# A planner's queue model, eight weight transfers and four chunk sizes in a fused attention and MLP kernel

## The chip, the cores and the metric

The kernel runs on one core of a Trainium2 chip. The metric is the device time in microseconds (us) of one execution. Five engines work side by side, each on its own stream of instructions in a fixed order: TensorE (PE: matmuls, with weight loads shown apart as PEld), VectorE (DVE), ScalarE (ACT), GpSimd (POOL) and SyncE (SP). SP computes nothing here; it issues transfers. Transfers issued by SP, ACT or POOL land later and announce it by semaphores. An instruction whose input is late holds up all that stand behind it on its engine.

## The reference

Inputs are q, k and v, each 8 batches x 8 heads x 576 positions x 64, in float32, and the MLP weights w_ch1 (512 x 2048) and w_ch2 (2048 x 512). Per head:

```
scores = q @ k.T / sqrt(64) + slope_h * (-|i - j|)
scores = where(0 <= i - j < 128, scores, -1e9)
attn   = softmax(scores) @ v
```

Heads are joined to x of 8 x 576 x 512, and then

```
xn  = (x - mean) / sqrt(var + 1e-6) * g_ln
out = x + relu(xn @ w_ch1) @ w_ch2
```

## The kernel before, in words

The 8 x 576 rows are 36 blocks of 128 positions. A block sees its own 128 keys and those of the block before. Nine blocks (`PERIOD`) make two batches; block 4 of the nine holds the end of one batch and the start of the next, so its q, k and v come as two half loads each.

For each block `attention(i)` records tasks. The names below are those that the prediction uses.

- SP loads q, k and v (256 KB each, `load`, L273) into rings of five buffers.
- POOL casts them to fp16: `cq`, `ck` (L369) and `cv` (L382).
- `T`: PE transposes q and k (L391), `ev` copies the result out of PSUM (L399 on DVE, L401 on ACT). From block `QK_BY_DMA` on, a DMA transpose issued by SP, `QT` (L406), stands for both.
- `S`: the scores (L426). For blocks below `BY_BIAS`, `Z` (L441) first writes the distance bias and the mask into PSUM by matmuls with a scaled identity; other blocks are masked after the exponential by `mk` (L472), a multiplication with a table.
- `ex`: the exponential on ACT (L465). `pv`: probabilities times v in two halves, `pva` and `pvb` (L489). `rc` and `nm` divide by the row sums (L505, L509), and `bn`, `ag` and `xs` give the normalised input of the MLP (L526 to L537).
- `TX`: PE transposes xs (L549), and `xt` copies it (L557, L559). From `X_BY_DMA` on, a DMA transpose `XT` (L564) stands for both.

Blocks are gathered in chunks (`CHUNKS`). For chunk c, `mlp(c)` records sixteen groups `Ac.f` of four matmuls each (L598; 128 columns of the moving operand per block of the chunk), each followed by a relu (L608 or L610), and then, for every block, four groups `Bi.0`, `Bi.4`, `Bi.8` and `Bi.12` of four matmuls (L624), `o` (L632), which adds x, and the output transfer (L640). Group `Ac.f` needs weight piece w(f // 4). Group `Bi.f` needs piece w(4 + f // 4). The eight pieces (L347, L349) are transfers that POOL issues, of 512 KB each as written, with a cast from float32. The PSUM banks `fb0` to `fb3` are shared by T, pv, TX, A and B.

The order of all instructions is not written by hand. `Plan.run` (L69) plays the tasks through a model of the engines. Each task has a guessed cost, dependencies and a due value `v`; `av(i, stage)` gives attention its due values. The order in which tasks start in the model is the order in which they are emitted, and so the order on every engine. Costs and times of the model are guesses and are not used as times in this text. A dependency that is named to the planner sets the order; only true data dependencies become semaphores. Before the change all transfers share one modelled queue `DMA`, one after the other, and a piece of weights may be issued as soon as a named load (`W_AFTER`) has landed in the model.

While the modelled start of a PE task is below `WARM` = 26, `keep_warm` (L651) fills the modelled gaps of PE with matmuls on a tile of zeros (L653).

Of the kernel before, what the change touches and what calls it, by code (L numbers as in the profile page):

```python
# [15 lines left out]
class Task:  # L16
    __slots__ = ("eng", "emit", "deps", "v", "lat", "acq", "rel", "left", "users", "ready", "end", "start", "name")

    def __init__(self, name, eng, emit, deps, v, lat, acq, rel):
        self.name, self.eng, self.emit, self.v, self.lat = name, eng, emit, v, lat  # L20
        self.deps = [d for d in deps if d is not None]
        self.acq, self.rel = acq, rel
        self.users, self.ready, self.end, self.start = [], 0.0, None, None

# [21 lines left out]
class Plan:  # L46


    def __init__(self):
        self.tasks, self.rings, self.banks, self.opens = [], [], {}, {}  # L50
# [5 lines left out]

    OVERLAP = {"ACT": 0.10, "DVE": 0.07, "POOL": 0.05}

    def add(self, name, eng, emit, deps=(), v=0.0, lat=None, acq=None, rel=None):
        if not isinstance(eng, dict):  # L60
            eng = dict([eng])
        if lat is None:
            lat = 0.2 if "PE" in eng else 0.05 + max(self.OVERLAP[e] for e in eng)
        eng = {e: c - self.OVERLAP.get(e, 0.0) for e, c in eng.items()}
        t = Task(name, eng, emit, deps, v, lat, acq, rel)
        self.tasks.append(t)
        return t

    def run(self):  # L69
        for r in self.rings:  # L70
            r.link()
        for t in self.tasks:
            t.left = len(t.deps)
            for d in t.deps:
                d.users.append(t)
        engines = sorted({e for t in self.tasks for e in t.eng})
        free = dict.fromkeys(engines, 0.0)
        avail = {e: [] for e in engines}
        for t in self.tasks:
            if t.left == 0:  # L80
                for e in t.eng:
                    avail[e].append(t)
        state = {p: {b: self.opens.get((p, b), 0.0) for b in bs} for p, bs in self.banks.items()}
        held, waits = {}, {}
        for t in self.tasks:
            if t.rel is not None:
                waits[t.rel] = waits.get(t.rel, 0) + 1
        order = []

        def at(t):  # L90
            if t.acq is None or t.acq[1] in held:
                return t.ready, None
            open_ = [(when, b) for b, when in state[t.acq[0]].items() if when is not None]
            if not open_:
                return None, None
            when, b = min(open_)
            return max(t.ready, when), b

        left = len(self.tasks)
        while left:  # L100
            best = None
            for e in engines:
                f = free[e]
                cand = []
                for t in avail[e]:
                    r, b = at(t)
                    if r is None:
                        continue
                    s = max(r, f)
                    if any(max(r, free[o]) + c < s + t.eng[e] - 1e-9 for o, c in t.eng.items() if o != e):  # L110
                        continue
                    cand.append((s, t.v, t, b))
                if not cand:
                    continue
                s = min(c[0] for c in cand)
                c = min((c for c in cand if c[0] <= s + 1e-9), key=lambda c: (c[2].v > -9e3, c[2].ready) if e == "DMA" else c[1])
                if best is None or (s, c[1]) < (best[0], best[1]):
                    best = (s, c[1], e, c[2], c[3])
            if best is None:
                raise RuntimeError("plan is stuck: " + ", ".join(t.name for e in engines for t in avail[e])[:600])  # L120
            s, _, e, t, b = best
            for o in t.eng:
                avail[o].remove(t)
            t.start, t.end = s, s + t.eng[e]
            free[e] = t.end
            if t.acq is not None and t.acq[1] not in held:
                held[t.acq[1]] = (t.acq[0], b)
                state[t.acq[0]][b] = None
            if t.rel is not None:
                waits[t.rel] -= 1  # L130
                if waits[t.rel] == 0:
                    p, hb = held[t.rel]
                    state[p][hb] = t.end + t.lat
            order.append((t, e, held[t.acq[1]][1] if t.acq is not None else None))
            left -= 1
            for u in t.users:
                u.ready = max(u.ready, t.end + t.lat)
                u.left -= 1
                if u.left == 0:
                    for o in u.eng:  # L140
                        avail[o].append(u)
        self.held = held
        self.order = order
        return order


@with_exitstack
def kernel(
# [10 lines left out]
    nc = tc.nc  # L159
# [4 lines left out]
    P = 128  # L164
# [7 lines left out]
    CH = CB * P  # L172
    CHUNKS = [3, 3, 2, 4, 4, 4, 4, 4, 4, 4]
    FIRST = [sum(CHUNKS[:c]) for c in range(len(CHUNKS))]
# [26 lines left out]
    WARM = 26.0  # L201
    PICK = {('xt', 0): 'ACT DVE', ('xt', 8): 'ACT DVE', ('cv', 5): 'ACT', ('cv', 0): 'POOL', ('ev', 8): 'DVE ACT', ('ev', 1): 'ACT', ('mkb', 8): 'POOL', ('mkb', 3): 'DVE', ('mka', 2): 'POOL'}
    G_AT = 1.3
    BY_BIAS = 4
    MASK_AT = 4
    QK_BY_DMA = 14
    X_BY_DMA = 14

    plan = Plan()
# [58 lines left out]

    def dma(name, eng, issue, secs, emit, deps=(), v=0.0):
        t = add(name + ".i", (eng, issue), emit, deps, v, lat=0.0)  # L270
        return t, add(name, ("DMA", secs), None, [t], -1e4 if eng == "POOL" else v, lat=2.0)

    def load(name, src, r, i, v):  # L273
        got = []
        for p0, n, b, s0 in where(i):
            def emit(e, bank, p0=p0, n=n, b=b, s0=s0):
# [3 lines left out]
                )  # L280
            t, d = dma(f"{name}{i}", "SP", 0.6, 1.22 * n / P, emit, (), v)
            r.writes(i, t)
# [7 lines left out]
    for t in vx.tiles:  # L290
        nc.vector.memset(t[:, :, D:VD], 1.0)

    d_iden = dma("iden", "ACT", 0.5, 0.15, lambda e, b: nc.scalar.dma_start(out=iden, in_=iden_dram.ap()), (), -1e6)[1]
    d_dist = dma("dist", "ACT", 0.5, 0.45, lambda e, b: nc.scalar.dma_start(out=dist_t, in_=dist_dram.ap()), (), -9e5)[1]
    d_g = dma(
        "g", "SP", 0.6, 0.8,
        lambda e, b: nc.sync.dma_start(out=g_t, in_=moe_g_ln.unsqueeze(0).broadcast_to([P, d_model])), (), av(G_AT) - 300,
# [3 lines left out]
    for h in range(H):  # L301
        def emit(e, b, h=h):
            nc.vector.tensor_scalar(out=sid[:, h, :], in0=iden[:, :], scalar1=-float(slopes[h] / inv_sqrt_d), scalar2=None, op0=ALU.mult)
# [36 lines left out]

    W_AFTER = [11, 14, 14, 17, 17, 17, 17, 17]
    t_w1, t_w2 = [], []
    for n, i in enumerate(W_AFTER):
        def emit(e, b, n=n):
            m = n % 4
            if n < 4:
                nc.gpsimd.dma_start(out=w1sb[:, :, 512 * m : 512 * m + 512], in_=w1r[:, :, 512 * m : 512 * m + 512])  # L347
            else:
                nc.gpsimd.dma_start(out=w2sb[:, 4 * m : 4 * m + 4, :], in_=w2r[:, 4 * m : 4 * m + 4, :])  # L349
        (t_w1 if n < 4 else t_w2).append(dma(f"w{n}", "POOL", 0.8, 3.25, emit, loads[i // 3][i % 3], av(i / 3, -60.0))[1])  # L350

    qkt_done, vx_done, aggr_done, xs_done, xt_done = {}, {}, {}, {}, {}

    def attention(i):
# [28 lines left out]
        cv = add(f"cv{i}", pick("cv", "POOL", POOL=0.64, ACT=0.62), e_cv, lv_, av(i, 0.2))  # L383
        v32.reads(i, cv); vx.writes(i, cv)

        if i < QK_BY_DMA:
# [17 lines left out]
        else:  # L404
            def e_td(e, b):
# [3 lines left out]
                )  # L409
            ti, ev = dma(f"QT{i}", "SP", 1.0, 1.1, e_td, [cq, ck], av(i, -4.0))  # L410
            qk16.reads(i, ev)
# [150 lines left out]
        else:  # L562
            def e_xd(e, b):
                nc.sync.dma_start_transpose(out=xt[c][:, :, j * P : j * P + P], in_=xs[i][:, :])  # L564
            xi, xt_ = dma(f"XT{i}", "SP", 1.0, 0.6, e_xd, [xs_], av(i, 7.0))
            xs.reads(i, xt_)
# [19 lines left out]
    def mlp(c):  # L586
# [5 lines left out]
        for f in range(NFB):  # L592
# [3 lines left out]
            def e_a(e, b, f=f):  # L596
                for kb in range(NKB):
# [3 lines left out]
                    )  # L601
            a = add(key, ("PE", 0.216 * nb), e_a, done + [t_w1[f // 4]], vm, acq=("fb", key))
            xt.reads(c, a)
# [10 lines left out]
        for j in range(nb):  # L614
# [3 lines left out]
            for f0 in range(0, NFB, 4):  # L618
                vm = v0 + 16 * per + (4 * j + f0 / 4) * SPAN / 32

                def e_b(e, b, j=j, f0=f0, key=key):
                    pm = fb[plan.held[key][1]]
                    for f in range(f0, f0 + 4):
# [3 lines left out]
                        )  # L627
                last = add(f"{key}.{f0}", ("PE", 0.864), e_b, relu[f0 : f0 + 4] + [t_w2[f0 // 4], last], vm, acq=("fb", key))
                ht.reads(c, last)
# [9 lines left out]
            def e_d(e, b, i=i):  # L639
                nc.sync.dma_start(out=out_flat[i * P : i * P + P, :], in_=ot[i][:, :])  # L640
            t, d = dma(f"out{i}", "SP", 0.6, 0.8, e_d, [o], vm - 4.0)
            ot.reads(i, d)
# [51 lines left out]
```

## Time and profile before

| what | value |
|---|---|
| median of 7 runs | 335.32 us (334.0 to 335.88) |
| the profiled execution | 334.71 us, of it 332.9 us of span |
| PE busy | 318.1 us, 96% of the span |
| DVE, ACT, POOL busy | 56%, 47%, 24% |
| granted PE clock over the span | 0.985 |
| MLP product one (L598) / two (L624) | 135.3 us / 132.2 us of PE |
| weight pieces, from issue to landing | w_ch1 8.0 us, w_ch2 14.3 us (medians of 4) |
| q, k, v loads of 256 KB, from issue to landing | 4.6, 4.8, 5.0 us (medians) |

The profile is of one execution; the span runs from its first to its last instruction. PE is busy nearly throughout, but its warm-up matmuls count as busy too, and a matmul at half clock is busy for twice as long. Tables by stretch tell more than the share of the whole. In a timeline row the columns are the start, the duration, the engine, the line, the operation, what it writes and reads, and how many; in brackets stands the idle time of the engine ahead of it, and what ended it.

### The profile page before, as it was taken

Reading aid. Unit: us, or ns where it says so; the run is one execution under the profiler, and the core shown is the slowest. Engines: PE = TensorE matmul, PEld = TensorE weight load, DVE = VectorE, ACT = ScalarE, POOL = GpSimd, SP = SyncE. Lnnn points to the kernel's source line nnn. Section 1 sums busy time; section 2 is a strip of 40 time slices with the busy share of each in tenths; the row PEclk is TensorE's granted clock in tenths of the full one; section 3 lists DMA queues with packets and bytes.
Section 4 is the critical chain, followed back from the end, with each engine's and each line's share of the span. In section 5 each row is a group of like instructions: output and inputs, shape, how many; then the busy total and the mean of one; then the engine's idle time right before and its main releaser. Section 6 shows DMA issues by size and latency. Waiting matters only on the chain.

```text
span 332.9 us, 6829 instructions
## 1 busy us (share of the span) xinstructions
PE 318.1 (96%) x2695; PEld 175.1 (53%) x2695; DVE 187.0 (56%) x403; ACT 156.6 (47%) x253; POOL 80.9 (24%) x127
## 2 busy tenths in 40 slices
PE   8996499999899999999999999999999999999994
PEld 8883355565586454554544444444445445444442
DVE  1597530389897655865666666666656655511011
ACT  4444362284383583457326722772277327505600
POOL 3881701507632213250131232132000000000000
PEclk9999599999999999999999999999999999999999
DMA  9999999998999999999999997623422320121011
GB/s 184 220 177 215 187 196 211 207 270 181 210 249 223 205 233 178 247 198 223 192 222 198 199 163 194 144 49 97 123 51 56 104 81 18 25 70 63 2 63 63
DMA packets 157584, 51.54 MB, mean 155 GB/s; under 512 B 148592, under 2 KB 152816, under 8 KB 157552
## 3 DMA queue, kind: packets, MB, share of 16 engines
q1 hardware_dynamic: 153040, 46.68, 69.3%
q0 software_dynamic: 4224, 4.19, 7.6%
q8 instruction: 21, 0.34, 0.5%
q10 hardware_dynamic: 288, 0.23, 0.2%
q14 instruction: 11, 0.09, 0.1%
HBM read 37.19 MB, written 9.44 MB: 140 GB/s over the span
## 4 chain that ended last, share of the span: by engine, by line
PE 87%; DVE 7%; DMA 4%; issue 1%; POOL 0%; DVEq 0%; POOLq 0%
PE fb L598 38%; PE fb L624 35%; PE sc L426 5%; PE fb L489 4%; DMA k<-in_k_dram 4%; PE fb L653 3%; DVE xs L537 2%; DVE st L526 1%; PE fb L391 1%; DVE xb L509 1%; PE fb L549 1%; DVE qkt L399 1%; DVE probs L472 1%; DVE ot L632 0%; PE sc L441 0%
## 5 line engine op out<-in xcount | busy, mean ns | idle before, releaser
L598 PE MATMUL fb<-xt,w1sb 128*128 128x512 f16 (+2 forms) x640 | 135.3, 361 | 0.2 <-DMA w1sb<-in_moe_w_ch_dram 0.2
L624 PE MATMUL fb<-w2sb,ht 128*128 128x512 f16 x576 | 132.2, 379 | 0.0
L610 ACT ACTIVATE ht<-fb 128x512 f16<-128x512 f32 (+2 forms) x145 | 80.4, 558 | 83.0 <-PE fb L598 82.3
L465 ACT ACTIVATE probs<-sc 128x1024 f16<-128x1024 f32 (+1 forms) x72 | 67.8, 973 | 52.5 <-PE sc L426 52.4
L598 PEld LDWEIGHTS <-w1sb 128*128 128x128 f16 x640 | 59.9, 98 | 57.0 <-issue 1.2
L624 PEld LDWEIGHTS <-ht 128*128 128x128 f16 x576 | 53.5, 98 | 59.2
L632 DVE SCALAR_TENSOR_TENSOR ot<-fb,rstd,xb 128x512 f32<-128x512 f32 x36 | 27.0, 749 | 68.7 <-PE fb L624 68.0
L382 POOL CAST vx<-v 128x512 f16<-128x512 f32 x35 | 22.0, 631 | 112.6 <-PE fb L489 96.2
L472 DVE TENSOR_TENSOR probs<-probs,mreg 128x1024 f16<-128x1024 f16 (+1 forms) x47 | 31.5, 675 | 18.1 <-ACT probs L465 17.9
L369 POOL CAST qk<-q 128x512 f16<-128x512 f32 x36 | 24.3, 674 | 37.5 <-issue 18.3
L509 DVE TENSOR_TENSOR xb<-fb,rec 128x256 f16<-128x256 f32 x72 | 30.2, 422 | 2.1
L537 DVE SCALAR_TENSOR_TENSOR xs<-xb,mv,g_t 128x512 f16<-128x512 f16 x36 | 29.8, 827 | 1.1
L489 PEld LDWEIGHTS <-probs 128*128 128x128 f16 x544 | 24.1, 98 | 11.6 <-DVE probs L472 0.8
L489 PE MATMUL fb<-vx,probs 128*128 128x65 f16 x544 | 26.8, 194 | 0.4 <-POOL probs L472 0.2
L369 POOL CAST qk<-k 128x512 f16<-128x512 f32 x36 | 23.7, 657 | 14.6 <-DMA k<-in_k_dram 14.5
L526 DVE BATCH_NORM_STATS2 st<-xb 128x6 f32<-128x512 f16 x36 | 24.9, 691 | 0.8
L505 DVE RECIPROCAL rec<-fb 128x4 f32<-128x4 f32 x72 | 12.7, 177 | 18.3 <-PE fb L489 17.9
L426 PEld LDWEIGHTS <-qkt 64*128 64x128 f16 x544 | 15.7, 95 | 11.7 <-issue 10.8
L426 PE MATMUL sc<-qkt 64*128 64x128 f16 x288 | 19.7, 219 | 0.0
L426 PE MATMUL sc<-qkt,qkt 64*128 64x128 f16 x256 | 18.4, 221 | 0.8 <-DVE qkt L399 0.8
L653 PE MATMUL fb<-warm_t 128*128 128x128 f16 x191 | 14.9, 240 | 1.0 <-DVE warm_t L288 1.0
L391 PE MATMUL fb<-iden,qk 128*128 128x128 f16 x112 | 9.1, 222 | 5.3 <-POOL qk L369 5.1
(35 smaller groups left out, 106.0 us busy)
## 6 DMA issues: line engine op xcount, KB each, us to landing
out_dram<-ot SPq DMA_DIRECT2D x36, 256.0 KB, 3.2
q<-in_q_dram SPq DMA_DIRECT2D x32, 256.0 KB, 4.6
k<-in_k_dram SPq DMA_DIRECT2D x32, 256.0 KB, 4.8
v<-in_v_dram SPq DMA_DIRECT2D x32, 256.0 KB, 5.0
w1sb<-in_moe_w_ch_dram POOLq DMA_DIRECT2D x4, 512.0 KB, 8.0
w2sb<-in_moe_w_ch_dram POOLq DMA_DIRECT2D x4, 512.0 KB, 14.3
q<-in_q_dram SPq DMA_DIRECT2D x8, 128.0 KB, 4.1
k<-in_k_dram SPq DMA_DIRECT2D x8, 128.0 KB, 3.6
```

The lines of the kernel that those rows point to most:

```text
L369: en.tensor_copy(out=qk16[i][:, a, :], in_=s)
L426: nc.tensor.matmul(scs[half][:, g, c0 : c0 + P], kt[rows, 1, hp, :], qkt[i][rows, 0, hp, :], start=not bias, stop=True, skip_group_check=True,
L465: nc.scalar.activation(out=o, in_=n_, func=AF.Exp, scale=inv_sqrt_d)
L472: en.tensor_tensor(out=pv, in0=pv, in1=mask[:, 2 * half : 2 * half + 2, :, lo:], op=ALU.mult)
L489: nc.tensor.matmul(pp[:, hh * (D + 1) : hh * (D + 1) + D + 1], probs[i][:, bank, slot, side * P : side * P + P], vx[i - 1 + side][:, h, 0 ...
L509: nc.vector.tensor_tensor(out=xb[i][:, 256 * half : 256 * half + 256].rearrange("p (h d) -> p h d", d=D), in0=pp[:, :, 0:D], in1=rec[2 * i ...
L526: nc.vector.bn_stats(out=st[i][:, :], in_=xb[i][:, :])
L537: nc.vector.scalar_tensor_tensor(out=xs[i][:, :], in0=xb[i][:, :], scalar=mv[c][:, j, 0:1], in1=g_t[:, :], op0=ALU.subtract, op1=ALU.mult,)
L598: nc.tensor.matmul(fb[b][:, 0:n_], w1sb[:, kb, f * P : f * P + P], xt[c][:, kb, 0:n_], start=(kb == 0), stop=(kb == NKB - 1),)
L610: nc.scalar.activation(out=ht[c][:, f, 0:n_], in_=src, func=AF.Relu)
L624: nc.tensor.matmul(pm[:, :], ht[c][:, f, j * P : j * P + P], w2sb[:, f, :], start=(f == 0), stop=(f == NFB - 1),)
L632: nc.vector.scalar_tensor_tensor(out=ot[i][:, :], in0=fb[plan.held[key][1]][:, :], scalar=rstd[c][:, j : j + 1], in1=xb[i][:, :], op0=ALU. ...
```

## The change

The planner's model of transfers is replaced. Each issuing engine has its own modelled queue, and queues that are active together share the rate by fixed parts. A transfer waits for room in its queue. The simulation steps through time with a heap of events, where before it chose the earliest start. `transfer` takes the place of `dma` at all call sites, with new costs:

```diff
+    QUEUE_ROOM = 4.0
+    LANDING = 2.0
...
+    def transfer(self, name, eng, issue, secs, room, emit, deps=(), v=0.0):
+
+        i = self.add(name + ".i", (eng, issue), emit, deps, v, lat=0.0)
+        d = self.add(name, ("DMA " + eng, secs), None, [i], v, lat=self.LANDING)
+        i.room = d.room = room
+        return i, d
+
+    def rates(self, queues):
+        on = [q for q, x in queues.items() if x]
+        if "DMA POOL" in on and len(on) > 1:
+            return {q: 0.92 if q == "DMA POOL" else 0.17 / (len(on) - 1) for q in on}
+        return {q: 1.0 / len(on) for q in on}
...
-    def dma(name, eng, issue, secs, emit, deps=(), v=0.0):
-        t = add(name + ".i", (eng, issue), emit, deps, v, lat=0.0)
-        return t, add(name, ("DMA", secs), None, [t], -1e4 if eng == "POOL" else v, lat=2.0)
...
-            t, d = dma(f"{name}{i}", "SP", 0.6, 1.22 * n / P, emit, (), v)
+            t, d = plan.transfer(f"{name}{i}", "SP", 0.6, 1.22 * n / P, n / P, emit, (), v)
...
-            ti, ev = dma(f"QT{i}", "SP", 1.0, 1.1, e_td, [cq, ck], av(i, -4.0))
+            ti, ev = plan.transfer(f"QT{i}", "SP", 1.4, 1.4, 1.0, e_td, [cq, ck], av(i, -4.0))
...
-            xi, xt_ = dma(f"XT{i}", "SP", 1.0, 0.6, e_xd, [xs_], av(i, 7.0))
+            xi, xt_ = plan.transfer(f"XT{i}", "SP", 1.2, 0.85, 0.5, e_xd, [xs_], av(i, 7.0))
...
-            t, d = dma(f"out{i}", "SP", 0.6, 0.8, e_d, [o], vm - 4.0)
+            t, d = plan.transfer(f"out{i}", "SP", 0.42, 0.8, 0.12, e_d, [o], vm - 4.0)
```

The core of the new loop:

```diff
+            for e in engines:
+                if free[e] > now + 1e-9:
+                    continue
+                best = None
+                for t in avail[e]:
+                    if best is not None and t.v >= best[0].v:
+                        continue
...
+                    if t.room and used["DMA " + e] + t.room > self.QUEUE_ROOM:
+                        continue
...
+            rate = self.rates(queues)
+            ends = [(now + queues[q][0][1] / r, q) for q, r in rate.items()]
...
+            nxt = min([x[0] for x in ends] + ([max(now, heap[0][0])] if heap else []))
+            for q, r in rate.items():
+                queues[q][0][1] -= (nxt - now) * r
```

The weight pieces are tied to casts in place of loads, and each comes after the piece before it. The constants change too:

```diff
-    W_AFTER = [11, 14, 14, 17, 17, 17, 17, 17]
...
-        (t_w1 if n < 4 else t_w2).append(dma(f"w{n}", "POOL", 0.8, 3.25, emit, loads[i // 3][i % 3], av(i / 3, -60.0))[1])
+    W_AFTER = [8, 14, 15, 15, 16, 17, 17, 18]
+    t_w = {}
+
+    def weights(i, casts):
+
+        for n, at in enumerate(W_AFTER):
+            if at // 3 != i:
+                continue
...
+            last = [t_w[n - 1][0]] if n else []
+            t_w[n] = plan.transfer(f"w{n}", "POOL", 0.8, 3.2, 0.0, emit, [casts[at % 3]] + last, av(i, -60.0))
...
         v32.reads(i, cv); vx.writes(i, cv)
+        weights(i, (cq, ck, cv))
...
-    CHUNKS = [3, 3, 2, 4, 4, 4, 4, 4, 4, 4]
+    CHUNKS = [2, 3, 4, 3, 4, 4, 4, 4, 4, 4]
...
-    PICK = {('xt', 0): 'ACT DVE', ('xt', 8): 'ACT DVE', ('cv', 5): 'ACT', ('cv', 0): 'POOL', ('ev', 8): 'DVE ACT', ('ev', 1): 'ACT', ('mkb', 8): 'POOL', ('mkb', 3): 'DVE', ('mka', 2): 'POOL'}
+    PICK = {('xt', 0): 'ACT DVE', ('xt', 8): 'ACT DVE', ('cv', 5): 'ACT', ('cv', 0): 'POOL ACT', ('ev', 8): 'DVE ACT', ('ev', 1): 'ACT', ('mkb', 8): 'POOL', ('mkb', 3): 'POOL', ('mka', 2): 'DVE', ('mkb', 4): 'POOL'}
     G_AT = 1.3
-    BY_BIAS = 4
-    MASK_AT = 4
-    QK_BY_DMA = 14
+    BY_BIAS = 6
+    MASK_AT = 6
+    QK_BY_DMA = 12
     X_BY_DMA = 14
```

An entry n of `W_AFTER` names block n // 3 and its q, k or v by n % 3. In the built order of the changed kernel POOL's stream from the first piece on reads cq4, w0, cq3, ck3, cv3, ck4, cv4, w1, cq5, w2, w3, ck5, w4, w5, w6, cq6, w7, ck6, cv6; before it read ck3, w0, cv3, cq4, ck4, w1, w2, cv4, cq5, ck5, w3 to w7, cq6, ck6, cv6. SP's loads read g, half of q4, q2, k2, v2, the other half of q4, half of k4, q3, k3, v3, the rest of k4, v4, then q5 and on; before, block after block. PE's order from the first MLP group reads A0.0, A0.1, TX2, pva3, A0.2, pvb3, Z4, T4, A0.3, S4, TX3, T5, pva4, pvb4, Z5, S5, A0.4; before, A0.0 to A0.3, pva4, TX3, pvb4, T5, S5, TX4, A0.4.

## The prediction

> **What bounds the kernel now.** I read the page's head first, then the busy time by stretch, then TensorE's timeline in the one stretch that looks bad, then the queues that feed it.
>
> ```profile
> span 332.9 us, 6829 instructions
> PE 318.1 (96%) x2695; PEld 175.1 (53%) x2695; DVE 187.0 (56%) x403; ACT 156.6 (47%) x253; POOL 80.9 (24%) x127
> ```
> ```profile
> 0.00:26.00 26.00, 24.24 (x403) 22.25 (x403) 14.04 (x47) 12.26 (x21) 16.45 (x28) 1.00 1.04 197
> 26.00:43.00 17.00, 9.49 (x82) 6.04 (x83) 9.88 (x20) 6.73 (x10) 8.14 (x11) 0.70 1.12 197
> 43.00:61.00 18.00, 18.00 (x109) 9.56 (x107) 3.11 (x8) 7.12 (x16) 3.17 (x6) 1.00 1.18 207
> 61.00:92.00 31.00, 29.58 (x327) 18.11 (x326) 25.70 (x55) 16.73 (x27) 15.50 (x21) 1.00 1.00 218
> 92.00:143.00 51.00, 51.00 (x463) 29.41 (x461) 36.01 (x76) 27.42 (x47) 12.92 (x22) 1.00 1.10 222
> 143.00:329.00 186.00, 185.78 (x1321) 89.73 (x1319) 97.70 (x200) 86.34 (x134) 24.73 (x41) 1.00 0.56 112
> ```
>
> The columns after each stretch are PE, PEld, DVE, ACT, POOL, granted clock, DMA share, GB/s. TensorE (PE) is the bound, and full from 92 us to the last matmul at 328.8; 4.1 us of tail follow. An order can gain only ahead of 92: the fill before 26 (mostly warm-up matmuls, L653), 26 to 43 (9.5 busy of 17, clock 0.70), and about 1.4 us idle in 61 to 92. A clock of 0.70 over 17 us is 0.30 x 17 x 2 = 10.2 us at half speed.
>
> ```profile
> 26.20 2.77 PE L598 MATMUL fb<-xt,w1sb 128*128 128x384 f16 x16 [0.24 <-DMA w1sb<-in_moe_w_ch_dram]
> ...
> 30.34 0.39 PE L391 MATMUL fb<-iden,qk 128*128 128x128 f16 x4
> 35.85 0.61 PE L391 MATMUL fb<-iden,qk 128*128 128x128 f16 x4 [5.13 <-POOL qk L369]
> 37.31 0.29 PE L426 MATMUL sc<-qkt,qkt 64*128 64x128 f16 x2 [0.85 <-DVE qkt L399]
> ...
> 39.20 0.60 PE L549 MATMUL fb<-iden,xs 128*128 128x128 f16 x4 [0.86 <-DVE xs L537]
> 39.60 2.77 PE L598 MATMUL fb<-xt,w1sb 128*128 128x384 f16 x8
> ```
>
> Four MLP groups of chunk 0 run, then the transpose of block 5 (T5) stands in order ahead of everything and waits for the cast of k5. MLP resumes at 39.6, at half clock until 43. The reason lies on POOL and SP:
>
> ```profile
> 23.07 1.48 POOL L347 DMA_DIRECT2D w1sb<-in_moe_w_ch_dram  x2
> 27.26 0.61 POOL L382 CAST vx<-v 128x512 f16<-128x512 f32 x1 [2.71 <-DMA v<-in_v_dram]
> 27.99 0.90 POOL L369 CAST qk<-q 128x512 f16<-128x512 f32 x1
> 35.19 0.61 POOL L369 CAST qk<-k 128x512 f16<-128x512 f32 x1 [6.30 <-DMA k<-in_k_dram]
> ```
> ```profile
> 44.53 6.59 SPq L277 DMA_DIRECT2D q<-in_q_dram  x1
> ...
> 57.45 0.94 SPq L277 DMA_DIRECT2D q<-in_q_dram  x1
> ```
>
> Weight pieces 1 and 2 were issued at 23.1, ahead of k5's bytes. Counting packets by queue, in 38 to 54 us the weights move 155 GB/s and SP's loads 38; alone, SP moves 218 (row 61 to 92), 1.2 us for 256 KB. With weights on the wire a load takes 6.6 to 6.9 us, as SP's issue row shows. k5's last packet came at 33.0, its cast 2.2 us later (others 0.8 to 2.3; I take 1.6).
>
> **The change, part by part.** [...]Built orders say what stands behind what; durations are from this trace.
>
> *w0.* SP now carries three half loads of block 4 ahead of block 3 (0.6 us each), g_t as before. By packets v2 landed at 14.5; now 15.1, q4 complete 15.7, v3 18.0 + 1.8 = 19.8. POOL issues w0 behind cv2 and cq4: 15.1 + 1.6 = 16.7, two casts of 0.6, so 17.9 (before 19.2). Issue to landing was 7.0 us for w0: A0.0 at 24.9 instead of 26.2. The next casts move behind it: ck3 ends 20.8, T3 about 21 (before 20.3), within the warm-up fill.
>
> *w1 to w7.* w0's bytes hold the wire about 20.3 to 24.3, so v4's last half lands at 24.6, q5 25.8, k5 27.0, v5 28.2. w1 is now behind cv4: 24.6 + 1.6 + 0.6 = 26.8; bytes about 2 us later, 28.8: k5 is through by 1.8 us. POOL then runs w1 (0.74), cq5, w2, w3, ck5: ck5 ends 30.3. So T5 stands at 30.3 instead of 35.85. Price: w1 lands 26.8 + 7.0 = 33.8 (before about 30). Pieces 4 to 7 landed 3.4 us apart (38.7 + 18.3 minus 36.5 + 10.4, over 3), so w2 37.2, w3 40.6, w4 44.0, w5 47.4, w6 50.8, w7 with its tail 55.1. The loads still under them: q6 about 32, k6 38.6, v6 45.4, q7 52.
>
> *PE, 24.9 to 62.* Chunk 0 has two blocks, so an A group costs 4 x 0.108 = 0.43 instead of 0.65. After A0.0: TX2, pv3, A0.1 to A0.3, Z4 (0.87), T4, S4, TX3, T5 at 30.3, pv4, Z5, S5 ending 33.2, then A0.4 when w1 lands, 33.8. Waits on the way are 0.3 to 1.4 us, with work between. From there in order: A0.4-7 with TX4, pv5, A1.0 to 36.9; A0.8 at 37.2; five groups, TX5, A1.2-3, A0.12-15, A1.4-5 to 44.1; B0.0, B1.0, A1.6, T6 (ck6 ready 40.8), S6, B0.4, B1.4, A1.8-9, B0.8, B1.8, A1.10, pv6 to 53.9; 1.2 us waiting for w7; B0.12, B1.12, A1.11 to A1.15, T7 (ck7 ready 56.3), TX6, S7, T8 to 62.1.
>
> *Sum at that point.* By 62.1 the changed kernel has done A0 6.9 + A1 10.4 + B0, B1 6.9 = 24.2 of MLP, and beyond block 5 also T6-8, S6-7, pv6, TX6 = 3.2. By 61.0 the old one had A0 10.4 + 5 x 0.65 + 9 x 0.863 = 21.4 and nothing beyond block 5. That is 6.0 us more work for 1.1 us more time: 4.9 ahead.
>
> *Smaller edits.* QK_BY_DMA 14 to 12 takes T12 and T13 off PE: 2 x 0.45 = 0.9 gained later. BY_BIAS 4 to 6 adds Z4, Z5 (1.74 us PE, already in the walk above) and removes four DVE masks of 0.7. cv0 on ACT, mkb3/mka2/mkb4: in the fill or inactive, 0; uncovered, one cast of 0.6.
>
> *What comes back later.* A chunk of 3 moves from the front to place 4 and PE runs MLP alone for longer (A2.12 to A3.5), while attention from block 12 waits for QT12, which stands on SP behind v20. From v20's landing of 111.5 before, minus two QTs and one output now behind it (3.5) and a 0.6 earlier start: about 107.5, QT12 109, usable 111; PE comes to S12 at about 113.5. So 0, or up to 2 if SP slips; I take 0.3. Blocks 12 to 17 then pass in some 24 us with 4.1 us of DVE each (masks 1.4, rc and nm 1.0, stats 0.9, xs 0.8) plus three outputs: DVE nearly full, as in 61 to 92, where PE lost 1.4. Between pvb15 and A4.0 PE has 7.9 us of work; DVE needs 3.5 to xs15 and its transfer 2.6 to 5.1: a wait of 0 to 1.5. I take 1.5 for both. The 61 to 92 stretch itself I leave at its loss. Sum: 4.9 + 0.9 - 1.8 = 4.0.
>
> Profiled execution 334.71 (span 332.9 + 1.8), so 330.7; the median of the runs shown is 0.6 higher, 335.32, so **331.3**.
>
> **Two rules of the Trainium skill against rows.** The row: DMA moves 197, 197, 207 GB/s in the first three stretches, so the wire is already full. "DMA: Bandwidth & Descriptors", § Issuing engines are not separate DMA queues, says that DMAs of several engines run on the same 16 engines and interleave; a second queue saves issue time only. By that, reordering moves no byte total earlier: w7 lands 55.1 against 57.0, a gain of 1.9. But old PE reaches B0.12 at 61.0, 4 us after w7, so arrival of the last byte is not what it waited for; the row of 5.13 us is, and I keep 4.9. Second, the same page, § Anatomy of one DMA, fits a GpSimd DMA as 2.0 us plus bytes/436e3: 512 KB would take 3.2 us, and w1 would stop mattering (A0.4 at 33.3, no wait for w7: 1.7 less, 329.6). The row says 7.0 and 3.4 per piece behind it; I use the row.
>
> **Rivals.**
> *A, nothing is given back.* DVE was 59% busy over 43 to 92 and copes, SP is on time: 331.3 - 1.8 = 329.5, or 328.5 if w1 also comes a microsecond sooner. Against it: the 1.4 us lost at 83% DVE in 61 to 92. 0.17.
> *B, slower: k5 misses the gap.* T5 depends on k5 being through before w1's bytes, 1.8 us of margin. If not, the rest of it moves at 38 GB/s: a whole load missed lands about 5.7 us later, T5 at 36, A0.4 near 40, and a PE wait that long drops the clock again (10.2 us at half, some 2 us of work), less the 1.5 of waits for weights that vanish: +6, 337.5. It decides at about 0.7 of a load missed. For it: old k5 did just that. Against: POOL cannot reach w1 before cv4. 0.14.
> *C, the hole moves to block 12.* Each microsecond by which QT12 is usable after 113.5 is lost whole; at 117.5 the gain is gone, at 119 the time is 336.8. For it: SP is full to 150 us. Against: 2.5 us of slack. 0.14.
>
> **How the numbers follow.** My case (0.55) runs 329.5 to 333.5: the later losses between 0 and 4. A run of this kernel tells about 0.3% (1 us) from none. Faster: my case, A, and 0.02 each of B and C's mild ends, 0.76; same 0.05; slower 0.19. The range goes from A's better end, 328.0, to 336.5, inside B and C: about 0.04 below, 0.12 above.
>
> **What would show it.** Right: w0 issued near 18 and w1 near 27; the cast of k5 ending near 30, no 5 us wait at the transposes of block 5; clock 1.00 through 26 to 43; A0.4 near 34; T8 near 62; PE idle at S12 or A4.0 under 2. Wrong: PE waiting at T5 or S5 for POOL, a second half-clock stretch, w1 after 35, or several microseconds of PE idle at the first scores of 110 to 120.

## The result, and the profile after

The changed kernel takes 331.87 us (median of 12 runs, 329.88 to 334.16); the kernel before takes 334.91 us (31 runs). The ratio is 0.9908, with a 95% interval of 0.9885 to 0.9932: 3.0 us faster. The prediction was 331.3. The profiled execution has a span of 329.8 us; before it was 332.9.

The head of the page of the changed kernel:

```profile
span 329.8 us, 6816 instructions
PE 318.8 (97%) x2701; PEld 175.7 (53%) x2701; DVE 184.2 (56%) x402; ACT 155.0 (47%) x249; POOL 80.8 (25%) x126
```

PE's busy time has hardly moved (318.1 before), for its sum also counts warm-up matmuls and doubles what runs at half clock. The stretches tell more (the columns are those of the table of before: PE, PEld, DVE, ACT, POOL, granted clock, DMA share, GB/s):

```profile
26.00:43.00 17.00, 15.35 (x187) 12.27 (x188) 12.48 (x32) 8.32 (x16) 8.62 (x13) 0.90 1.19 194
43.00:61.00 18.00, 17.87 (x141) 10.71 (x139) 6.47 (x14) 8.33 (x17) 3.69 (x6) 1.00 1.18 208
61.00:92.00 31.00, 29.96 (x301) 17.04 (x299) 27.29 (x57) 17.06 (x28) 18.13 (x23) 1.00 1.17 235
92.00:143.00 51.00, 49.93 (x414) 26.39 (x413) 28.84 (x65) 22.67 (x36) 10.59 (x19) 1.00 1.14 214
```

From 26 to 43 PE was busy for 9.49 us at a clock of 0.70; it is now busy for 15.35 at 0.90, so 0.10 x 17 x 2 = 3.4 us are at half clock where there were 10.2. In 92 to 143, where nothing was idle before, 1.07 us now are. PE's timeline at the front (start, duration, then the idle time ahead in brackets):

```profile
26.52 1.89 PE L657 MATMUL fb<-xt,w1sb 128*128 128x256 f16 x8 [2.56 <-DMA w1sb<-in_moe_w_ch_dram]
...
33.24 0.61 PE L450 MATMUL fb<-iden,qk 128*128 128x128 f16 x8
...
36.39 1.48 PE L657 MATMUL fb<-xt,w1sb 128*128 128x256 f16 x12
```

The second row is T5: the wait of 5.13 us in front of it is gone. The third is A0.4; ahead of it S5 ends and, at 36.35, piece w1 lands. What let T5 come earlier is POOL's order:

```profile
18.47 0.93 POOL L404 DMA_DIRECT2D w1sb<-in_moe_w_ch_dram  x1
...
26.98 0.61 POOL L427 CAST qk<-k 128x512 f16<-128x512 f32 x1 [4.57 <-issue]
28.43 0.61 POOL L440 CAST vx<-v 128x512 f16<-128x512 f32 x1 [0.83 <-DMA v<-in_v_dram]
28.99 0.75 POOL L404 DMA_DIRECT2D w1sb<-in_moe_w_ch_dram  x1
29.73 0.62 POOL L427 CAST qk<-q 128x512 f16<-128x512 f32 x1
30.28 1.48 POOL L404 DMA_DIRECT2D w1sb<-in_moe_w_ch_dram  x2
31.75 0.63 POOL L427 CAST qk<-k 128x512 f16<-128x512 f32 x1
```

Piece w1 goes at 28.99, behind cv4, and ck5 ends at 32.38; before, two pieces went at 23.07 and ck5 ended at 35.80.

To compare kernels whose orders differ I use one sum for each trace. At a given time, take what PE has done by then of real work, each kind at its full-clock duration (a matmul of 512 columns 0.216 us, the others about in proportion, and less for those of the scores, which start in pairs), and subtract it from the time. What is left is lost: fill, warm-up matmuls, idle time, and the half of a half-clock stretch. In us:

| kernel | lost by 43 | by 61 | by 100 | by 160 | at the end | PE work | last matmul |
|---|---|---|---|---|---|---|---|
| before | 26.2 | 26.7 | 29.2 | 29.9 | 31.0 | 297.6 | 328.6 |
| after | 21.4 | 21.8 | 23.5 | 26.0 | 27.2 | 298.5 | 325.7 |

The change loses 4.9 less by 61. Of this it spends 0.9 on more PE work (Z4 and Z5 +1.74, T12 and T13 -0.90), and 1.1 is lost again later. That leaves 2.9, and the spans differ by 3.1.

### The profile page after: what moved, and what is told of

It is laid out like the page before. It is cut to its first block, busy times and chain, and to the rows that moved or that the text cites. A ratio compares the mean times of both kernels' runs of the same rounds, so it can differ in the third digit from the quotient of the medians.

```text
span 329.8 us, 6816 instructions
## 1 busy us (share of the span) xinstructions
PE 318.8 (97%) x2701; PEld 175.7 (53%) x2701; DVE 184.2 (56%) x402; ACT 155.0 (47%) x249; POOL 80.8 (25%) x126
## 4 chain that ended last, share of the span: by engine, by line
PE 83%; SPq 6%; DMA 5%; DVE 4%; issue 1%; POOL 0%; ACT 0%; POOLq 0%
PE fb L657 37%; PE fb L683 36%; SPq L329 5%; PE sc L485 5%; PE fb L548 4%; DMA w1sb<-in_moe_w_ch_dram 3%; DMA v<-in_v_dram 3%; DVE probs L531 1%; PE fb L608 1%; DVE ot L691 1%; DVE xb L568 1%; DVE xs L596 1%; PE fb L450 0%; DVE st L585 0%; DVE qkt L458 0%
## 5 line engine op out<-in xcount | busy, mean ns | idle before, releaser
L531 DVE TENSOR_TENSOR probs<-probs,mreg 128x1024 f16<-128x1024 f16 (+1 forms) x47 | 31.8, 683 | 25.0 <-ACT probs L524 24.9
L427 POOL CAST qk<-q 128x512 f16<-128x512 f32 x36 | 23.3, 647 | 54.9 <-DMA qkt<-qk 41.8
L548 PE MATMUL fb<-vx,probs 128*128 128x65 f16 x544 | 26.8, 194 | 1.5 <-DVE probs L531 1.1
L427 POOL CAST qk<-k 128x512 f16<-128x512 f32 x36 | 23.6, 654 | 17.6 <-DMA k<-in_k_dram 11.0
L585 DVE BATCH_NORM_STATS2 st<-xb 128x6 f32<-128x512 f16 x36 | 24.9, 690 | 0.8
L485 PEld LDWEIGHTS <-qkt 64*128 64x128 f16 x544 | 15.4, 94 | 11.1 <-issue 10.2
L485 PE MATMUL sc<-qkt 64*128 64x128 f16 x288 | 19.4, 216 | 0.0
L458 DVE COPY qkt<-fb 128x1024 f16<-128x1024 f16 x11 | 7.5, 682 | 13.1 <-ACT ht L669 6.7
```

The lines of the kernel that those rows point to most:

```text
L427: en.tensor_copy(out=qk16[i][:, a, :], in_=s)
L485: nc.tensor.matmul(scs[half][:, g, c0 : c0 + P], kt[rows, 1, hp, :], qkt[i][rows, 0, hp, :], start=not bias, stop=True, skip_group_check=True,
L531: en.tensor_tensor(out=pv, in0=pv, in1=mask[:, 2 * half : 2 * half + 2, :, lo:], op=ALU.mult)
L548: nc.tensor.matmul(pp[:, hh * (D + 1) : hh * (D + 1) + D + 1], probs[i][:, bank, slot, side * P : side * P + P], vx[i - 1 + side][:, h, 0 ...
L585: nc.vector.bn_stats(out=st[i][:, :], in_=xb[i][:, :])
```

## The experiments

The theory was that the weights' place does it: k5's bytes pass ahead of w1, and T5 no longer waits. The rivals were that the chunks of 2, 3, 4, 3 do it, that it is the shares of the engines (`BY_BIAS`, `MASK_AT`, `QK_BY_DMA`), and that the clock does it. Two parts of the change were not tried alone: the new order of SP's loads and the new entries of `PICK`.

### One part alone, and one part undone

In the kernel before, w1 and w2 are moved in the finished order, behind ck5; all else stays.

```diff
+    def move(name, behind):
+        t = next(x for x in order if x[0].name == name)
+        order.remove(t)
+        order.insert(1 + next(n for n, x in enumerate(order) if x[0].name == behind), t)
+    move("w1.i", "ck5")
+    move("w2.i", "w1.i")
```

> The kernel before with one edit: on POOL weight pieces 1 and 2 are issued directly behind the cast of block 5's k instead of directly behind that of block 4's. Theory (the 5.1 us wait of PE at block 5's transpose is the price of weights sent ahead of k5): k5 lands near 28.5, its cast ends near 30.5, T5 stands near 30.5 instead of 35.9. The wait then moves to piece 1, issued at 30.4 and landed near 37.4: A0.4 at 37.5 instead of 39.6, perhaps at half clock again, so 1 to 3 us faster than before, 332 to 334. Rival (chunk sizes and shares make the gain, the place of the weights does not): T5 moves but the time stays at 335 within 1 us, since the same bytes pass the same wire.

Measured: 333.78 us, ratio 0.9986 (0.9958 to 1.0014); span 330.8. PE's timeline and the stretch of 26 to 43:

```profile
30.50 0.61 PE L391 MATMUL fb<-iden,qk 128*128 128x128 f16 x8
32.47 0.23 PE L426 MATMUL sc<-qkt,qkt 64*128 64x128 f16 x2 [1.37 <-DVE qkt L399]
...
34.08 0.40 PE L549 MATMUL fb<-iden,xs 128*128 128x128 f16 x4 [0.98 <-DVE xs L537]
36.84 2.74 PE L598 MATMUL fb<-xt,w1sb 128*128 128x384 f16 x8 [2.37 <-DMA w1sb<-in_moe_w_ch_dram]
```
```profile
26.00:43.00 17.00, 11.53 (x107) 7.07 (x102) 11.24 (x24) 7.73 (x12) 10.14 (x13) 0.80 1.17 189
```

T5 moves to 30.50, earlier than in the changed kernel, but a lump of waits now ends at A0.4, which w1 holds up, and A0.4 to A0.6 run at half clock. The trace is ahead by 2.1 us, but it is of the fastest of the twelve runs (332.61 us). The timed runs don't resolve a gain: by the interval it is 1.4 us at most. So the weights' place alone opens T5 but is worth less than half of what the whole change gains.

In the changed kernel the same two pieces are moved the other way, behind cv3:

```diff
+    move("w1.i", "cv3")
+    move("w2.i", "w1.i")
```

> The changed kernel with one edit: pieces 1 and 2 are issued directly behind cv3, ahead of ck4 and cv4, near 22.4 to 24 us. Theory: their 6.8 us of bytes follow piece 0 at once, and the rest of block 4 and block 5 pass at 38 GB/s; T5 moves from 33.2 to 38 or later, PE waits long enough to drop its clock, 4 to 7 us slower than the changed kernel: 336 to 339. Rival (chunk sizes and shares make the gain): within 1 us of the changed kernel, 331 to 333.

Measured: 336.62 us, ratio 1.0056 (1.0032 to 1.0080), 4.7 above the changed kernel. Its stretch and its timeline:

```profile
26.00:43.00 17.00, 11.74 (x144) 9.33 (x143) 9.58 (x24) 5.55 (x9) 6.99 (x11) 0.80 1.09 193
```
```profile
34.37 0.41 PE L450 MATMUL fb<-iden,qk 128*128 128x128 f16 x4 [3.11 <-POOL qk L427]
36.29 0.61 PE L450 MATMUL fb<-iden,qk 128*128 128x128 f16 x4 [1.51 <-POOL qk L427]
...
40.38 1.88 PE L657 MATMUL fb<-xt,w1sb 128*128 128x256 f16 x11
```

The wait at T5 is back, 4.6 us in two parts, and A0.4 stands 4.0 later than in the changed kernel. T5 moved to 36.3, less far than the 38 that was expected. The pieces stand one cast earlier here than in the kernel before, where they followed ck4, so the edit does more than put back the old place. In this order, then, all of the gain hangs on the weights coming late enough, and the first run says that this isn't sufficient.

### The chunks and the shares

Each is set back in the changed kernel, and the planner lays its order anew:

```diff
-    CHUNKS = [2, 3, 4, 3, 4, 4, 4, 4, 4, 4]
+    CHUNKS = [3, 3, 2, 4, 4, 4, 4, 4, 4, 4]
```

> The changed kernel with the old chunk sizes 3, 3, 2, 4, laid anew by the new planner. POOL's and SP's orders up to block 9 stay as they are. Theory (weights behind casts): T5 stays near 33, A0.4 near 36.5, clock as in the changed kernel; three-block groups keep PE busy under the arriving weights; 331.5 to 334. Rival (the small first chunk makes the gain): A0.0 must wait for block 2, chunk 1 is complete only with block 5, PE starves between the pieces: 334.5 to 337. The later order differs too, so the stretches are to be compared, 0 to 61 for this question.

Measured: 339.93 us, ratio 1.0157 (1.0125 to 1.0188). Stretches, then PE's timeline:

```profile
26.00:43.00 17.00, 15.77 (x187) 10.96 (x185) 13.23 (x31) 9.47 (x18) 7.40 (x11) 1.00 1.20 196
...
92.00:143.00 51.00, 46.91 (x409) 25.30 (x406) 27.59 (x65) 25.13 (x40) 12.71 (x21) 1.00 1.20 210
```
```profile
146.52 5.80 PE L657 MATMUL fb<-xt,w1sb 128*128 128x512 f16 x18 [3.74 <-DMA xt<-xs]
```

Both forecasts were too low. With the old chunks the front is as good or better: clock 1.00, and 19.4 lost by 61. Most of the time goes at 137 to 150, where PE waits for block 17's and 18's probabilities and then for a transposed block. From 143.3 to 150.1 its clock is at half, which costs the work from 146.5 on another 1.8 us.

```diff
-    BY_BIAS = 6
-    MASK_AT = 6
-    QK_BY_DMA = 12
+    BY_BIAS = 4
+    MASK_AT = 4
+    QK_BY_DMA = 14
```

> The changed kernel with BY_BIAS and MASK_AT back at 4 and QK_BY_DMA back at 14, laid anew by the new planner. Theory: only the sum's small terms go: T12 and T13 are back on PE (0.9 us), Z4 and Z5 leave it (1.7 us, but in the fill), four masks come back to DVE and POOL: 332.3 to 333.5. Rival (the shares make the gain): the masks of blocks 4 and 5 delay the front and the time goes back to 335.

Measured: 339.11 us, ratio 1.0116 (1.0074 to 1.0158), again above both forecasts.

```profile
27.57 1.05 PE L657 MATMUL fb<-xt,w1sb 128*128 128x256 f16 x8 [3.37 <-DMA w1sb<-in_moe_w_ch_dram]
...
35.03 0.42 PE L548 MATMUL fb<-vx,probs 128*128 128x65 f16 x8 [0.67 <-DVE probs L531]
...
37.32 0.42 PE L548 MATMUL fb<-vx,probs 128*128 128x65 f16 x8 [1.08 <-POOL probs L531]
```

Lost by 61: 25.8. Part of it is w0, which landed at 27.52 in this execution (26.48 in the first profile of the changed kernel). Another part is what the rival named: with `BY_BIAS` and `MASK_AT` back at 4 PE waits for masks at the front, 2.3 us in three places up to 40.3. 6.3 more are lost between 100 and 160.

Both runs lose most where the prediction's rival C put the hole, at the blocks from 12 on. To see whether `QK_BY_DMA` is behind that, it is set to 16, so that PE transposes blocks 12 to 15 itself (1.8 us of work), with the changed kernel's chunks and with the old ones:

```diff
-    QK_BY_DMA = 12
+    QK_BY_DMA = 16
```

> The changed kernel with QK_BY_DMA 16 alone. Theory: the 2 us lost by PE at 115 to 142 shrink to under 0.7, the four transposes on PE cost 1.8 us: 331 to 332.5, the same as the changed kernel within 0.3%. Rival (those losses are of the DVE alone, whatever brings the transposes): 333 to 334.

> The changed kernel with the old chunk sizes 3, 3, 2, 4 and QK_BY_DMA 16, so that blocks 12 to 15 are transposed by PE. Theory (with old chunks the front is 2.5 us better than in the changed kernel, and the 11 us lost at 120 to 160 come from block 12 starting late behind the DMA transposes on SP, which packs the masks of blocks 14 to 18 onto a full DVE): the hole goes, PE pays 4 x 0.45 = 1.8 us for the transposes, and the time is 329.5 to 331.5. Rival (the hole comes from chunk sizes: fewer MLP groups are left to cover the attention): still 4 us or more lost at 120 to 160, 334 or more.

Measured: 331.93 us, ratio 0.9939 (0.9906 to 0.9972) with the chunks 2, 3, 4, 3, and 332.69 us, ratio 0.9981 (0.9942 to 1.0019) with the old ones. The row of 92 to 143, first of the one, then of the other:

```profile
92.00:143.00 51.00, 51.00 (x447) 28.06 (x446) 34.98 (x73) 23.69 (x39) 14.34 (x23) 1.00 1.14 215
```
```profile
92.00:143.00 51.00, 50.75 (x448) 28.15 (x446) 35.01 (x72) 24.81 (x41) 13.35 (x23) 1.00 1.11 216
```

With the old chunks, 47 us busy become 51: the hole at 137 to 150 goes when PE transposes blocks 12 to 15. By DMA the transposes stand on SP behind loads, and S12 starts at 115.1; here it starts at 103.4. That the late start packs these blocks' work on DVE into less time, and so makes the hole, fits but is not shown by itself. The time of 332.69 us is above the 329.5 to 331.5 that was expected. With the changed kernel's chunks the same edit saves 1.8 us of later losses and pays 1.8 us of PE work: no change against 331.87. The chunks, then, aren't what repairs the front; with them the later blocks come out better.

### The planner's model of the queues

All other parts of the change are kept, and the planner is the one of before, with one queue for all transfers. Against the changed kernel the edit reads, in part:

```diff
-            t_w[n] = plan.transfer(f"w{n}", "POOL", 0.8, 3.2, 0.0, emit, [casts[at % 3]] + last, av(i, -60.0))
+            t_w[n] = dma(f"w{n}", "POOL", 0.8, 3.25, emit, [casts[at % 3]] + last, av(i, -60.0))
...
+    def dma(name, eng, issue, secs, emit, deps=(), v=0.0):
+        t = add(name + ".i", (eng, issue), emit, deps, v, lat=0.0)
+        return t, add(name, ("DMA", secs), None, [t], -1e4 if eng == "POOL" else v, lat=2.0)
```

> The old planner with its single transfer queue, and all the other parts of the change: weights behind casts, chunk sizes 2, 3, 4, 3, BY_BIAS and MASK_AT 6, QK_BY_DMA 12, the new picks. Piece 1 stands directly behind cv4 here too; SP's loads come block by block. Theory (the place of the weights makes the gain, not the queue model): T5 near 32, the stretch up to 61 as in the changed kernel, 331 to 333.5. Rival (the new model of the queues is what makes it): 334 to 338, lost behind 61 us where orders of loads and transposes were laid from wrong times.

Measured: 336.27 us, ratio 1.0085 (1.0050 to 1.0120).

```profile
26.00:43.00 17.00, 12.00 (x129) 9.02 (x127) 10.60 (x25) 7.04 (x13) 8.03 (x12) 0.80 1.13 189
...
61.00:92.00 31.00, 28.43 (x298) 16.20 (x297) 29.13 (x60) 15.13 (x22) 16.52 (x22) 1.00 1.12 224
```
```profile
35.77 1.03 PE L605 MATMUL fb<-xt,w1sb 128*128 128x256 f16 x4 [2.50 <-DMA w1sb<-in_moe_w_ch_dram]
```

T5 is at 30.53: the weights' place works here too. But A0.4 then waits 2.50 us for w1, as in the first run, the clock drops to 0.80, and 3.8 us are lost in 61 to 100 where the changed kernel loses 1.7. The theory that the weights' place with any order around it gives the gain has fallen, and the time is in the rival's range. The order around the weights is needed, and this run doesn't say which part of the new planner makes it: each run that is laid anew differs from the others in hundreds of positions. The constants are those of the new planner; whether others suit the old one better was not tried.

### The clock

In the changed kernel, A0.0 waits 2.56 us and then runs at half clock. Warm-up matmuls fill that wait:

```diff
+                if t.name == "A0.0":
+                    keep_warm(0.0, 2.2)
```

> The changed kernel with 35 more warm-up matmuls (2.1 us at full clock) on PE directly ahead of A0.0, where PE stood idle 2.6 us until piece 0 landed. Theory (that idle stretch is what took the clock to half for 3.4 us after it, at a cost of about 1 us): clock 1.00 over 26 to 43, and 0.5 to 1.2 us faster than the changed kernel, 330.7 to 331.4. Rival (the drop costs nothing, since block 5 and piece 1 end the wait at A0.4 anyway): the clock is 1.00 and the time that of the changed kernel within 0.4 us.

Measured: 331.88 us, ratio 0.9946 (0.9915 to 0.9977), no gain against the changed kernel. The clock over 26 to 43 is 1.00, and yet by 43 the same 21.4 us are lost:

```profile
33.02 0.40 PE L608 MATMUL fb<-iden,xs 128*128 128x128 f16 x4 [0.72 <-DVE xs L596]
...
39.90 2.57 PE L657 MATMUL fb<-xt,w1sb 128*128 128x256 f16 x20 [0.49 <-DMA w1sb<-in_moe_w_ch_dram]
```

TX3 waits for xs3 until 33.02 (33.01 without the warm-ups), and A0.8 for w2, which landed at 39.86 (39.87). So the half clock at A0.0 was covered by later waits. One trace can't give its price: here w0 landed 0.6 later, and xs3 took 1.21 us, not 0.75.

The same in the kernel with w1 and w2 behind ck5, where the lump of waits ends at A0.4:

```diff
+                n = {"T5": 12, "S5": 16, "A0.4": 36}.get(t.name, 0)
+                for _ in range(n):
+                    to = scs[0][:, 0, 0:P] if t.name == "S5" else fb[b][:, 0:P]
+                    nc.tensor.matmul(to, warm_t[:, :], warm_t[:, :], start=True, stop=True, skip_group_check=True)
```

> The kernel before with pieces 1 and 2 behind the cast of k5, as in the first run, and 64 warm-up matmuls in the waits that this left on PE: 12 ahead of T5, 16 ahead of S5, 36 ahead of A0.4. Theory (in the first run what T5 gained was given back because the waits at T5 to A0.4 halved the clock for 6.8 us): clock 1.00, A0.4 at 36.5, and about 2 us less than the first run, so a span near 329, as fast as the changed kernel. Rival (A0.4 onwards is bound by the arriving weights, so a faster PE only waits more): the clock is 1.00 and the span that of the first run, 330.8, within 0.5 us.

Measured: 333.45 us, ratio 0.9971 (0.9938 to 1.0004).

```profile
34.12 2.17 PE L670 MATMUL fb<-warm_t 128*128 128x128 f16 x36
38.59 2.10 PE L598 MATMUL fb<-xt,w1sb 128*128 128x384 f16 x8 [2.29 <-DMA w1sb<-in_moe_w_ch_dram]
```

Here w1 landed at 38.54 (36.79 in the first run), and A0.4 waited for it another 2.29 us after the warm-ups; over 26 to 43 the clock was 0.90, not the 1.00 that both forecasts had. The time is that of the first run within 0.4 us. So that order is held by w1's landing, and neither run shows a gain from the clock.

The changed kernel once more, with no edit:

> The changed kernel once more, unedited, on the chip of the two runs beside it, as what they are compared with. All theories: 330.5 to 333, about 0.9% under the kernel before.

Measured: 332.03 us, ratio 0.9908 (0.9876 to 0.9940). The profiled span is 331.7, against 329.8 in the first profile of the same kernel:

```profile
26.00:43.00 17.00, 14.59 (x171) 11.68 (x172) 11.43 (x29) 6.71 (x13) 8.01 (x12) 0.80 1.05 187
```

Its w0 landed at 27.30, not at 26.48; A0.0 starts at 27.35, and 6.8 us run at half clock, not 3.4. By 43 it has lost 1.9 more, which is the whole difference of the spans.

### The later loss

What is lost at 138 to 140 in the changed kernel, on PE and then on DVE:

```profile
138.36 1.03 PE L657 MATMUL fb<-xt,w1sb 128*128 128x512 f16 x4
140.45 0.42 PE L548 MATMUL fb<-vx,probs 128*128 128x65 f16 x8 [1.06 <-DVE probs L531]
```
```profile
138.38 0.69 DVE L585 BATCH_NORM_STATS2 st<-xb 128x6 f32<-128x512 f16 x1
138.99 0.73 DVE L691 SCALAR_TENSOR_TENSOR ot<-fb,rstd,xb 128x512 f32<-128x512 f32 x1
139.64 0.17 DVE L590 BATCH_NORM_AGGREGATE mv<-st 128x2 f32<-128x6 f32 x1
139.73 0.66 DVE L531 TENSOR_TENSOR probs<-probs,mreg 128x1024 f16<-128x1024 f16 x1
```

pva17 waits for its mask, mka17, and this stands on DVE behind the statistics of block 16 and an output. The edit puts the mask ahead of the statistics:

```diff
+    move("mka17", "nm1.16")
+    for name, behind in (("bn16", "nm0.17"), ("ag16", "bn16"), ("xs16", "ag16")):
+        move(name, behind)
```

> The changed kernel with DVE's order edited at one place: the masks of block 17 come ahead of output 11, and the statistics and xs of block 16 behind the first half of block 17's division. Theory (PE's 1.2 us wait at pva17, 139 to 140, is the mask standing behind bn16 and o11 on a full DVE): the wait at pva17 goes, 0.8 to 1.4 us faster than the changed kernel on the same chip. Rival (the wait moves to the next group that needs DVE, pvb17 or A4.3): under 0.4 us of difference.

Measured: 336.42 us, ratio 1.0066 (1.0038 to 1.0094). This run says nothing on the theory's time: XT16 stood ahead of the moved xs16, so it transposed what the buffer held before (block 16's normalised input is left out of the MLP), and xs16 had to wait for that transfer. With the issue of XT16 moved too:

```diff
+    for name, behind in (("bn16", "nm0.17"), ("ag16", "bn16"), ("xs16", "ag16"), ("XT16.i", "xs16")):
+        move(name, behind)
```

> The changed kernel with DVE's order edited at one place: the masks of block 17 come ahead of output 11, and the statistics and xs of block 16 behind the first half of block 17's division, with the transpose of xs16 kept behind xs16. Theory (PE's 1.2 us wait at pva17, 139 to 140, is the mask standing behind bn16 and o11 on a full DVE): the wait goes, span 0.8 to 1.4 us under the changed kernel's at the same granted clock; against the kernel before a ratio near 0.987. Rival (the wait moves to the next group that needs DVE): PE loses as much between 137 and 145 as in the changed kernel, and the ratio stays at 0.991.

Measured: 330.08 us (6 runs), ratio 0.9874 (0.9831 to 0.9916), span 328.0.

```profile
137.94 1.03 PE L657 MATMUL fb<-xt,w1sb 128*128 128x512 f16 x4
138.81 0.41 PE L548 MATMUL fb<-vx,probs 128*128 128x65 f16 x8
139.05 1.02 PE L657 MATMUL fb<-xt,w1sb 128*128 128x512 f16 x4
```
```profile
92.00:143.00 51.00, 50.98 (x421) 27.18 (x420) 29.24 (x65) 23.60 (x38) 10.98 (x19) 1.00 1.12 216
```

The wait is gone, and 92 to 143 is full. Only 1.2 us are lost from 100 to 160, where the changed kernel lost 2.5. It is faster than the kernel before; against the changed kernel, run beside the same kernel before at 0.9908 (0.9876 to 0.9940), the intervals overlap, so that step rests on the trace.

The sums of all these traces but the one that transposed xs16 too early:

| kernel | lost by 43 | by 61 | by 100 | by 160 | at the end | PE work | last matmul |
|---|---|---|---|---|---|---|---|
| before, w1 and w2 behind ck5 | 24.4 | 24.6 | 27.2 | 27.8 | 28.9 | 297.6 | 326.5 |
| the same with warm-ups | 25.4 | 25.7 | 28.2 | 28.9 | 30.0 | 297.6 | 327.6 |
| after, w1 and w2 behind cv3 | 25.4 | 25.9 | 27.6 | 30.2 | 31.4 | 298.5 | 329.8 |
| after, old chunks | 19.2 | 19.4 | 22.2 | 33.4 | 34.6 | 298.5 | 333.0 |
| after, old shares | 25.0 | 25.8 | 28.5 | 34.8 | 36.0 | 297.6 | 333.6 |
| after, `QK_BY_DMA` 16 | 22.5 | 22.9 | 24.9 | 25.6 | 26.7 | 300.2 | 326.9 |
| the same, old chunks | 20.1 | 20.3 | 23.8 | 24.9 | 26.0 | 300.2 | 326.2 |
| after, planner of before | 23.2 | 23.7 | 27.5 | 31.2 | 32.4 | 298.5 | 330.9 |
| after, warm-ups at A0.0 | 21.4 | 21.8 | 23.6 | 26.2 | 27.3 | 298.5 | 325.8 |
| after, once more | 23.3 | 23.7 | 25.4 | 27.9 | 29.1 | 298.5 | 327.6 |
| after, mask of 17 ahead | 20.9 | 21.3 | 23.1 | 24.3 | 25.4 | 298.5 | 323.9 |

## Why the prediction was right, step by step

- **The bound.** Right. The gain lies before 61, at T5, and the wait of 5.13 us there is gone.
- **w0.** Issued at 18.47 (said 17.9), A0.0 at 26.52 (24.9). The cover of A0.0 was called warm-up fill, but T3 and S3 ended near 23.5, only five warm-ups followed, and PE stood for 2.56 us. Of the 1.6 us 0.6 are the issue; landing took the rest, 8.0 us where 7.0 were said: w0 landed at 26.48, later than before (26.15), though it was issued 0.7 earlier.
- **w1.** Issued at 28.99 (26.8), because half of k4 stood on SP ahead of v4: it landed at 26.87, v4 only at 28.31, and cv4 ended at 29.04. This is the mis-sized term: 2.2 us. The 3.4 us from w1's issue to the end of ck5 were as said (3.5), so ck5 ended at 32.38 instead of 30.3. T5 stood at 33.24 instead of 30.3 (before 35.85), but ck5 had then been done for 0.86 us: what PE had ahead of it was last, A0.0 late by 1.6 and at half clock, then TX3, which waited for xs3 until 33.01. A0.4 came at 36.39 instead of 33.8 (before 39.60). It was to start when w1 lands, and w1's landing at 36.35, 7.4 us after its issue (7.0 by the row, 3.2 by the second rule), is 0.04 ahead of it; but S5 ended there too. In the second profile w1 landed at 37.11 and S5 was last, with A0.4 at 38.51. (w1 landed at 31.4 before, not near 30.)
- **The margin of k5.** The prediction called 1.8 us between k5 and w1's bytes, and made its slower rival B of the case that k5 misses them. Both shifted together, since w1 waits for cv4 in POOL's order. The run with the pieces behind cv3 shows B's mechanism: T5 done with its waits at 36.29, 336.62 us (B said 36 and 337.5).
- **The clock.** Said 1.00 over 26 to 43; it was 0.90, and 0.80 in the second profile.
- **w7.** Said 55.1, measured 56.97, which is also when it landed before: as the first of the two rules would have it, the new order moved no total of bytes earlier. B0.12 starts at 57.01, right behind the landing, but PE was busy until then, so the wait of 1.2 us that was said is gone. That gave back some of what was lost at the front.
- **The sum at T8.** Said 62.1, measured 64.0. The 6.0 us of work beyond the old order are done in 3.0 us more time than the old 61.0, not 1.1: 3.0 ahead instead of 4.9. This count leaves out Z4 and Z5. The sum of lost time counts their 1.74 us as work, and its 4.9 by 61 less 1.74 is the same 3.
- **Smaller edits.** The 0.9 of T12 and T13 came as said, and Z4 and Z5 cost what the walk had in it.
- **What comes back later.** Said 1.8, measured about 1.1. S12 starts at 114.32 with no wait (QT12 landed at 109.5, usable at 111 was said), so rival C did not come. A wait of up to 1.5 was named at A4.0, for block 15's transfer. A4.0 starts at 138.36 without one; the wait stands one group behind it, at pva17, and its cause is block 17's mask on DVE: moving that mask takes it away. That its size fits the forecast is luck. In 61 to 92 PE lost 1.04, before 1.42.

So the answer came out 0.6 us from the median by errors of opposite sign, and that close by luck: the front was over-estimated by 1.9 and the later losses by about 0.7. Of the gain of 4.0 that was said, 3.0 were measured. The distance in time is smaller because the sum starts from a median of 335.32 for the kernel before, which came to 334.91 with more runs. A second profile of the same kernel, 1.9 us longer, shows that executions differ by more than these distances.

One claim behind the sum was too simple. I took the gain to follow from the weights' place. The runs show that alone it gives 2.1 us in one trace and nothing that the timed runs resolve, with a lump of waits at A0.4 and half clock; weights sent early in the changed kernel cost 4.7. The rest comes with an order in which PE's waits are short and spread (0.35 us or so each between 29 and 36). With the planner of before and the same constants that order did not come, and the time was 336.27 us. Whether the model with one queue for each engine makes it by design, or it happens to come out of it, stays open: the same planner with old chunks makes a better front and a later hole of 11.2 us, and with old shares a worse front.

## What to carry to other kernels

A large transfer in chunks on a second queue can slow the small loads under it more than its own bytes say (here from 218 GB/s to 38 beside 155), so hold it behind the last load that the bottleneck engine needs soon, and look at who waits for the held piece next: a wait that moves whole to another place returns most of the gain (here with warm-ups in it, 333.45 us, and without, 333.78). Where an order is laid by a planner, changing one constant moves waits everywhere; test it by moving single tasks in the finished order as well, and sum the lost time of the bottleneck engine stretch by stretch.

## What was not expected of the hardware

- **The split of the wire.** With weight pieces in flight POOL's queue moved 155 GB/s and SP's loads 38, while the packets in the trace ran nearly one for one (in the kernel before 314 and 311 start between 44 and 46 us; 1024 bytes against 256). The Trainium skill, "DMA: Bandwidth & Descriptors", § Queues, rings and completion order, says that a DMA engine takes turns between its queues packet by packet. The counts agree with that, and the bytes then follow the packets' sizes. The page puts several descriptors into a packet; whether a record of the trace is one or the other isn't shown, and no run here changed its size.
- **The clock as a step of 3.4 us.** Over 17 us the granted clock is 1.00, 0.90, 0.80 or 0.70 in these traces, which is 0, 1, 2 or 3 times 3.4 us at half. The Trainium skill, "TensorE: Matmul & The Clock Gate", § Part 1: The HAM clock gate, gives a free-running window of that length, and the traces agree with the length. How long a wait must be is not settled by its length here: ahead of A0.0, waits of 2.03 and 2.56 us were followed by one step, one of 3.32 by two, but one of 3.37 (old shares) by only one.
- **Executions of one kernel differ, in part by the steps.** In the runs of the kernel before that stood beside one set of experiments, spans had a mean of 333.3 at a clock of 0.985 (10 runs), 331.9 at 0.989 (8) and 329.6 at 0.993 (3); the other 14 lie at other clocks. The clock is not all of it: the 8 runs at 0.989 go from 329.6 to 332.9. One profile shows one of these, and a difference of 2 us between two single profiles is no evidence by itself.
